# Transposing x on TensorE instead of by DMA in the first gate of a fused attention, experts and cosine-MLP kernel

## The chip, the cores and the metric

The kernel runs on one core of one Trainium2 chip. The metric is the time of one launch on the device, in microseconds (us): the median of a few runs. The kernel before took 1233.31 us (three runs, 1232.27 to 1233.43). A separate, profiled execution gives the trace.

## The reference

Three stages, each feeding the next. Cut to what matters:

```python
# attention: B, H, S, D = 4, 8, 576, 64; only the 32 largest scores of a row count
scores = scale * q @ k.T
kth    = 32nd largest of each row
attn   = softmax(where(scores >= kth, scores, -1e9))
x      = (attn @ v) as 2304 rows of 512
# experts: 8 of them, one per row, and only for rows with x @ w_skip > 0
e_idx  = argmax(x @ w_gate);  gate_w = softmax(x @ w_gate)[e_idx]
x2     = x + gate_w * (relu(x @ w1[e_idx]) @ w2[e_idx])      # other rows: x2 = x
# MLP: 512 -> 2048 -> 512
h      = x2 @ w_in
out    = (h * cos(h)) @ w_out
```

`w_in` and `w_out` come as 64-bit floats.

## The kernel before, in words

**Two halves.** The four batch entries are worked as two pairs, g = 0 and g = 1, of 1152 rows each. A pair has 8 heads of 9 *tiles* of 128 query rows: 72 tiles, numbered n = 0 to 143 over both pairs. Heads are taken from 7 down to 0 and inside a head the tile j from 8 down to 0. After a pair's attention come its gate (`route`), its experts (`experts`) and its share of the MLP (`cosine`).

**One tile** (`attend`). TensorE makes 128 x 576 scores into a two-bank PSUM slot (L584). VectorE takes the largest of eight pieces (L593) and narrows them (L603, L605); ScalarE makes exponentials and two helper passes (L610, L614, L617); TensorE shifts the scores twice (L622); VectorE finds the 32nd largest (L630) and masks (L633); ScalarE and GpSimd split the weights into two half-precision parts (L636, L640, L641); a DMA transposes them (L644, on SP's queue); TensorE multiplies with v (L651 to L660). Every third tile VectorE divides and writes three tiles' columns of x (L672 to L674). x is one buffer `xs` of three parts: part 2 holds j = 8, 7, 6, part 1 j = 5, 4, 3, part 0 j = 2, 1, 0. So part 0 is ready last.

**PSUM.** Pair 0 has three score slots, pair 1 two. The third slot, `s2`, is given up after its last tile, 71, and cut into two banks, `half`, which the experts and the MLP use (`recut`).

**Head preparation** (`prep_head`). q, k and v of the next head are loaded by DMA, multiplied by 16 on GpSimd (L520), split into two half-precision parts (ScalarE, and GpSimd at L496) and transposed by DMA (L525). GpSimd also works on the 64-bit weights `w_in`, `w_out` (L438, L445, L448) while pair 0's attention runs.

**The gate** (`route`). For each of nine row tiles, j = 0 to 8, x is split into two half-precision parts (`transposed`: L688 on ScalarE, L690 on VectorE), transposed by a DMA on SP's queue (L693), and TensorE makes nine logits (L743). Then one chain of small VectorE, ScalarE and TensorE instructions (L764 to L819) makes a table of rows for each expert.

**Experts.** GpSimd gathers 128 rows for an expert from `x_d` (L856), TensorE multiplies (pair 0: `turn` L868, `first` L888, `second` L919, in 32-bit precision; pair 1: half-precision parts made at L847 and L849). Each weight block is 512 KB and loaded on SP's queue (L839). Pair 0 has four buffers for them. The results are scattered into `x2_d` (L932). `store_x` writes x twice: to `x_d`, from which rows are gathered, and to `x2_d`, which holds x2.

**MLP** (`cosine`). For each of nine row tiles: 192 matmuls for h (L986), five elementwise steps (L998 to L1008), 48 matmuls for the output (L1016), an eviction (L1025). Pair 0's part, here cosine 0, is worked in between the attention of pair 1 and in what is left open by the gate and the experts of pair 1; cosine 1 comes last.

**What sets the order.** Every instruction group is a unit with an engine, an estimated cost, a priority and dependencies (`Plan.add`). `Plan.run` plays the units on a model of the engines: whichever engine is free takes the unit of least priority number among those that are ready in the model. The instructions are written in that order, and each engine then works strictly in it. A cost or a priority that changes can thus move instructions anywhere.

```python
                if ready[e]:
                    t = free[e]
                elif pending[e]:
                    t = max(free[e], pending[e][0][0])
...
            _, u = heapq.heappop(ready[e])
            u.fn()
```

## Time and profile before

| | |
|---|---|
| median of three runs | 1233.31 us |
| profiled execution, its own time | 1231.46 us |
| span of its instructions | 1229.3 us |
| TensorE busy | 965.1 us (79%) |
| VectorE busy | 875.2 us (71%) |
| ScalarE busy | 805.8 us (66%) |
| GpSimd busy | 598.8 us (49%) |

The span is what the trace covers; 2.2 us of the profiled execution lie around it. Busy shares are averages over stages with different limits. By the trace, pair 0's attention lasts to about 403 us, the first gate to 455 us, the first expert multiplication is at 462 us, pair 1's attention ends at 844 us, the experts of pair 1 at 1003 us, and cosine 1 fills the rest.

### The profile page before, as it was taken

To read this page: it belongs to the slowest core of one execution; us is meant where nothing else is said; L and a number is where in the kernel's file an instruction comes from. 1 tells how busy PE (TensorE), PEld (TensorE's weight loads), DVE (VectorE), ACT (ScalarE), POOL (GpSimd) and SP (SyncE) were. 2 spreads that over 40 slices of the span, in tenths; PEclk is the share of its full clock that TensorE was granted. 3 is DMA by queue.
4 is the path that set the end of the run, shared out by engine and by line. 5 is a ranking of instruction groups with operands and counts; after the bars stand their busy time and mean duration, and the time that the engine had idled before them with its cause. 6 is when DMAs were issued, how large, how long until landed. Compare 5 with 4: busy or idle time off the path is not lost.

```text
span 1229.3 us, 27654 instructions
## 1 busy us (share of the span) xinstructions
PE 965.1 (79%) x9855; PEld 681.8 (55%) x9856; DVE 875.2 (71%) x3186; ACT 805.8 (66%) x1657; POOL 598.8 (49%) x591
## 2 busy tenths in 40 slices
PE   1565565656565569898987989987999999999996
PEld 0343343333343357666654767765776667777773
DVE  6898998979897786777778878885478862433221
ACT  5888888878775656556666978775377755644431
POOL 6988979989654434444444633432222321122221
PEclk9985556555675559999996999999999999999999
DMA  7677687678669969999997455469379951310100
GB/s 184 148 164 166 130 156 162 146 146 163 112 113 245 202 130 222 256 271 280 267 283 195 96 105 133 88 151 239 72 223 336 302 191 38 70 35 19 26 20 21
DMA packets 352629, 193.81 MB, mean 158 GB/s; under 512 B 270050, under 2 KB 323298, under 8 KB 352480
## 3 DMA queue, kind: packets, MB, share of 16 engines
q1 hardware_dynamic: 349920, 185.66, 64.4%
q0 software_dynamic: 2560, 6.28, 1.6%
q8 instruction: 79, 1.29, 0.4%
q14 instruction: 70, 0.57, 0.1%
HBM read 107.50 MB, written 18.35 MB: 102 GB/s over the span
## 4 chain that ended last, share of the span: by engine, by line
PE 32%; DMA 16%; issue 9%; DVE 8%; POOL 6%; ACT 4%; SPq 2%; POOLq 0%; DVEq 0%; ACTq 0%
DMA arena<-arena 11%; PE half L986 5%; PE quarter L986 5%; PE quarter L1016 4%; PE m_bank L1016 4%; PE half L1016 3%; POOL arena L641 2%; DMA arena<-in_k_dram 1%; PE s L584 1%; DMA arena<-in_v_dram 1%; PE s L622 1%; PE m_bank L986 1%; DVE arena L633 1%; DMA arena<-x_d,gidx 1%; DVE arena L593 1%
## 5 line engine op out<-in xcount | busy, mean ns | idle before, releaser
L986 PEld LDWEIGHTS <-win 128*128 128x128 f16 x3456 | 215.7, 99 | 51.6 <-issue 1.8
L593 DVE MAX8 arena<-s 128x8 f32<-128x72 f32 x1152 | 197.6, 223 | 30.5 <-PE s L584 30.0
L1008 POOL TENSOR_TENSOR arena<-arena 128x512 f16<-128x512 f32 x72 | 86.5, 1201 | 254.6 <-ACT arena L1007 213.8
L651 PE MATMUL o_bank<-arena 128*128 128x65 f16 (+1 forms) x640 | 100.1, 221 | 99.2 <-DMA arena<-arena 96.0
L584 PE MATMUL s<-arena 128*128 128x320 f16 (+7 forms) x800 | 130.1, 328 | 52.4 <-DVE arena L633 33.6
L641 POOL TENSOR_TENSOR arena<-arena 128x512 f16<-128x512 f32 x144 | 169.8, 1179 | 0.0
L633 DVE SCALAR_TENSOR_TENSOR arena<-s,kth,arena 128x576 f32<-128x576 f32 x144 | 116.6, 809 | 50.9 <-PE s L622 38.5
L651 PEld LDWEIGHTS <-arena 128*128 128x128 f16 (+1 forms) x640 | 71.9, 116 | 144.5 <-DMA arena<-arena 133.5
L1003 DVE SCALAR_TENSOR_TENSOR arena<-arena 128x512 f32<-128x512 f32 x72 | 52.1, 723 | 136.6 <-ACT arena L1000 136.6
L986 PE MATMUL half<-arena,win 128*128 128x128 f16 x2112 | 146.7, 221 | 0.7 <-DMA arena<-arena 0.4
L636 ACT ACTIVATE arena<-arena 128x576 f16<-128x576 f32 x144 | 97.6, 678 | 73.4 <-DVE arena L633 56.3
L584 PEld LDWEIGHTS <-arena 128*128 128x128 f16 (+1 forms) x800 | 86.0, 122 | 98.0 <-issue 51.0
L640 POOL TENSOR_TENSOR arena<-arena 128x64 f16<-128x64 f32 x144 | 47.9, 332 | 164.1 <-ACT arena L636 148.0
L1016 PE MATMUL m_bank<-wout,arena 128*128 128x512 f16 x480 | 126.5, 381 | 0.0
L610 ACT ACTIVATE arena<-s,arena 128x576 f32<-128x576 f32 x144 | 105.4, 732 | 13.8 <-POOL arena L641 9.7
L622 PE MATMUL s<-arena,minus 128*128 128x320 bf16 (+1 forms) x288 | 76.5, 358 | 48.3 <-ACT arena L610 28.3
L630 DVE MAX8 kth<-s 128x8 f32<-128x584 f32 x144 | 110.0, 764 | 1.1
L614 ACT ACTIVATE arena<-s,arena 128x576 bf16<-128x576 f32 x144 | 105.7, 734 | 2.4
L520 POOL TENSOR_SCALAR arena<-arena 128x576 f32<-128x576 f32 (+1 forms) x45 | 77.2, 1717 | 61.5 <-DMA arena<-in_v_dram 34.4
L1016 PEld LDWEIGHTS <-arena 128*128 128x128 f16 x864 | 75.5, 98 | 48.5 <-issue 0.3
L622 PE MATMUL s<-arena,plus 128*128 128x320 bf16 (+1 forms) x288 | 77.3, 361 | 30.6 <-DVE kth L630 25.6
L653 PE MATMUL o_bank<-arena 128*128 128x64 f16 (+1 forms) x640 | 98.8, 218 | 0.0
(184 smaller groups left out, 2363.6 us busy)
## 6 DMA issues: line engine op xcount, KB each, us to landing
arena<-in_moe_w_dram SPq DMA_DIRECT2D x128, 512.0 KB
arena<-in_moe_w_in_dram SPq DMA_DIRECT2D x16, 512.0 KB
arena<-in_moe_w_out_dram SPq DMA_DIRECT2D x16, 512.0 KB
x_d<-arena SPq DMA_DIRECT2D x8, 768.0 KB
arena<-arena SPq DMA_DIRECT2D x32, 144.0 KB
arena<-x_d SPq DMA_DIRECT2D x18, 256.0 KB
out_dram<-arena SPq DMA_DIRECT2D x18, 256.0 KB
arena<-in_q_dram SPq DMA_DIRECT2D x16, 256.0 KB
```

Of the source, the lines that this page charges most:

```text
L584: nc.tensor.matmul(S_[rows, o:o + n_], qT.ap[:, i, cols], kT.ap[:, kc:kc + n_], start=(i == 0 and o < 512), stop=(i == 1), skip_group_chec ...
L593: add("DVE", dve(sw), lambda i=i: nc.vector.max(cand.ap[:, 8 * i:8 * i + 8], S_[:, sw * i:sw * i + sw]), r=[s], w=[cand[i]], prio=pr - 0.5)
L610: lambda: nc.scalar.activation(p.ap, S_, AF.Exp, bias=M[:, 40:41], scale=ESC),
L614: lambda: nc.scalar.activation(r.ap, S_, AF.Relu, bias=M[:, 41:42], scale=ESC),
L622: nc.tensor.matmul(S_[:, o:o + n_], by, r.ap[:, o:o + n_], start=False, stop=True, skip_group_check=True)
L630: add("DVE", 0.68, lambda: nc.vector.max(kth[g][:, z:z + 8], s.ap), r=[s], w=[found[n], in_turn], prio=pr)
L633: add("DVE", 0.73, lambda: nc.vector.scalar_tensor_tensor(p.ap, S_, kth[g][:, z + 7:z + 8], p.ap, op0=OP.is_ge, op1=OP.mult), r=[s, found[ ...
L641: nc.gpsimd.tensor_tensor(pc.ap[:, S + ST:], p.ap[:, 0:SM], pc.ap[:, 0:SM], op=OP.subtract)
L651: nc.tensor.matmul(oj[rows, 0:D + 1], pT.ap[:, c, rows], vh[:, 5 * b + c, :], start=(c == 0), stop=False)
L653: nc.tensor.matmul(oj[rows, 0:D], pT.ap[:, c, rows], vl[:, 5 * b + c, :], start=False, stop=False)
L986: nc.tensor.matmul(view(ph.ap, 4, P)[:, f, :], win.ap[:, c, sw, f0:f0 + P], xv[:, sx, c, :], start=(n == 0), stop=(n == 3 * KD - 1))
L1016: nc.tensor.matmul(po.ap, gv[:, sg, fc % 4, :], wout.ap[:, fc, sw, :], start=(fc == 0 and n_ == 0), stop=(fc == NFF - 1 and n_ == 2))
```

## The change

The gate of pair 0 no longer transposes by DMA. A new function `turned` transposes the 32-bit x on TensorE, four 128 x 128 blocks into one of the two banks of the third score slot (`ring_t`), and ScalarE and VectorE make the two half-precision parts from PSUM. For that the slot is recut before the gate instead of after it. Both gates take their row tiles from j = 8 down. The second store of x (`x2_d`) gets a larger priority number. The first four weight blocks of pair 0's experts wait for the division of tile 38 instead of tile 65. And the multiplication by 16 on GpSimd becomes a tensor-by-tensor product with a column of sixteens, with a planned cost of 1.23 us (0.11 + 576 x 0.00195) instead of 0.72 us.

```diff
+    ring_t = Ring(half)
...
+    times = sb("times", [1])
+    nc.vector.memset(times, SQ)
...
             if not early:
-                add("POOL", 0.2 + n * D * 0.0009, lambda: nc.gpsimd.tensor_scalar(x, x, SQ, None, op0=OP.mult),
-                    w=[st], prio=prio)
+                add("POOL", gp(n * D), lambda: nc.gpsimd.tensor_tensor(x, x, times[:, :, None].to_broadcast([P, n, D]),
+                                                                       op=OP.mult), w=[st], prio=prio)
...
+    def turned(src, src_slot, prio):
+
+        bk, xT = ring_t.new(), r_xT[0].new()
+        v16 = as16(xT.ap, 2, KD, P)
+
+        def turn():
+            for c in range(KD):
+                nc.tensor.transpose(view(bk.ap, KD, P)[:, c, :], src[:, c * P:(c + 1) * P], ident)
+
+        add("PE", 0.6, turn, r=[src_slot], w=[bk], prio=prio)
+        add("ACT", act(DM, True), lambda: nc.scalar.activation(v16[:, 0], view(bk.ap, KD, P), AF.Copy, scale=SX),
+            r=[bk], w=[xT], prio=prio)
+        add("DVE", dve(DM), lambda: nc.vector.scalar_tensor_tensor(
+            v16[:, 1], view(bk.ap, KD, P), SX, v16[:, 0], op0=OP.mult, op1=OP.subtract),
+            r=[bk], w=[xT], prio=prio)
+        return xT, v16
...
-                    prio=prio + (0.0 if dst is x_d[g] else 10.0))
+                    prio=prio + (0.0 if dst is x_d[g] else 30.0))
...
-        for j in range(NJ):
-            xT, xv = transposed(xs.ap[:, j, :], xs[j // 3], prio, g)
+        for j in reversed(range(NJ)):
+            if g == 0:
+                xT, xv = turned(xs.ap[:, j, :], xs[j // 3], prio)
+            else:
+                xT, xv = transposed(xs.ap[:, j, :], xs[j // 3], prio, g)
...
-                r=[gate[n0 - 7]] if g == 0 else [], w=[st], prio=prio[0] - 5, lat=0.6, dma=1.5)
+                r=[gate[n0 - 34]] if g == 0 else [], w=[st], prio=prio[0] - 5, lat=0.6, dma=1.5)
...
+    recut(third_ps, [s2], half, "half", "right")
     store_x(0, n0 + 0.0)
     route(0, n0 - 10.0)
-    recut(third_ps, [s2], half, "half", "right")
```

In the new file the lines after the insertions are larger by 1 to 23: L593 becomes L596, L633 L636, L674 L677, L644 L647, L707 L727, L847 L870, L998 L1021, L1025 L1048; the new L711 and L713 are the two evictions of `turned`.

VectorE's order at the end of pair 0, before. `s_82` is the third score slot, `s_77` and `s_78` the first two; `kth_126` belongs to pair 0, `kth_127` to pair 1. Tile 71 ends with the first row, parts 1 and 0 of x with the two L674, and L690 is the split of row tiles j = 0 and 1:

```order
L633 SCALAR_TENSOR_TENSOR arena<-s_82,kth_126,arena 128x576
...
L674 TENSOR_TENSOR arena<-o_bank,arena 128x3x64
...
L633 SCALAR_TENSOR_TENSOR arena<-s_77,kth_127,arena 128x576
...
L633 SCALAR_TENSOR_TENSOR arena<-s_78,kth_127,arena 128x576
...
L674 TENSOR_TENSOR arena<-o_bank,arena 128x3x64
...
L690 SCALAR_TENSOR_TENSOR arena<-arena 128x512 x2
```

The same place in the change, up to the first instruction of the routing table (L790):

```order
L677 TENSOR_TENSOR arena<-o_bank,arena 128x3x64
...
L636 SCALAR_TENSOR_TENSOR arena<-s_82,kth_128,arena 128x576
...
L713 SCALAR_TENSOR_TENSOR arena<-half_4389,arena 128x512
L713 SCALAR_TENSOR_TENSOR arena<-half_4390,arena 128x512
L636 SCALAR_TENSOR_TENSOR arena<-s_77,kth_129,arena 128x576
...
L636 SCALAR_TENSOR_TENSOR arena<-s_78,kth_129,arena 128x576
...
L677 TENSOR_TENSOR arena<-o_bank,arena 128x3x64
...
L790 TENSOR_SCALAR act_0_137<-lt_0_136 128x9
```

Six of the nine L713 now stand ahead of the division of part 0, and the last three, with the masks of tiles 74 and 75, between it and L790. In the order before the first expert multiplication on TensorE follows the scores of tile 83; in the change it follows those of tile 78.

SP's queue at the same place, before. The rows L644 are the transposes of tiles 70 to 73, `x_d_57` is the first store of x, `x_d` the second (`x2_d`):

```order
L644 DMA_TRANSPOSE arena<-arena 128x9x128
L707 DMA x_d_57<-arena 64x512 x2
L711 DMA x_d_57<-arena 128x512 x2
L644 DMA_TRANSPOSE arena<-arena 128x9x128
L707 DMA x_d<-arena 64x512 x2
L711 DMA x_d<-arena 128x512 x2
L644 DMA_TRANSPOSE arena<-arena 128x9x128
L716 DMA x_d_57<-arena 128x1536
L644 DMA_TRANSPOSE arena<-arena 128x9x128
L716 DMA x_d<-arena 128x1536
L693 DMA_TRANSPOSE arena<-arena 128x8x128 x2
```

And in the change, from tile 70's transpose on:

```order
L647 DMA_TRANSPOSE arena<-arena 128x9x128
L727 DMA x_d_57<-arena 64x512 x2
L731 DMA x_d_57<-arena 128x512 x2
L727 DMA x_d<-arena 64x512 x2
L731 DMA x_d<-arena 128x512 x2
L647 DMA_TRANSPOSE arena<-arena 128x9x128 x2
L736 DMA x_d_57<-arena 128x1536
L736 DMA x_d<-arena 128x1536
```

The second store of part 1 now stands ahead of tile 71's transpose, not behind it. The first four expert weight blocks stand between the transposes of tiles 67 and 70 before, and between those of tiles 39 and 41 in the change.

ScalarE's order behind the last split of an expert weight of pair 1 (L847, L870), where cosine 0 ends and cosine 1 begins, before (L998 starts the elementwise steps of a block of h, L688 splits a row tile of cosine 1, L1025 evicts a finished output):

```order
L847 ACTIVATE arena<-arena 128x1024 x3
L998 ACTIVATE arena<-half_4369 128x512
L1000 ACTIVATE arena<-arena,cbias 128x512
L1007 ACTIVATE arena<-arena 128x512
L998 ACTIVATE arena<-half_4368 128x512
...
L688 ACTIVATE arena<-arena 128x512 x2
...
L998 ACTIVATE arena<-half_4369 128x512
...
L1025 ACTIVATE arena<-m_bank 128x512
L1007 ACTIVATE arena<-arena 128x512
L1025 ACTIVATE arena<-m_bank 128x512
```

And in the change:

```order
L870 ACTIVATE arena<-arena 128x1024 x3
L691 ACTIVATE arena<-arena 128x512
L1048 ACTIVATE arena<-m_bank 128x512
L691 ACTIVATE arena<-arena 128x512
L468 ACTIVATE arena<-win_131 128x512 x3
```

Of cosine 0, three blocks of h and two outputs were still to do there; one output is left in the change. On TensorE the counts are 108 L986 and 78 L1016 behind the experts' last multiplication before, and no L986 and 39 L1016 in the change.

## Rows read from the trace of the kernel before

**Rows 1.** The page: span, TensorE's busy time, granted clock in 40 slices.

```profile
span 1229.3 us, 27654 instructions
PE 965.1 (79%) x9855; PEld 681.8 (55%) x9856; DVE 875.2 (71%) x3186; ACT 805.8 (66%) x1657; POOL 598.8 (49%) x591
PEclk9985556555675559999996999999999999999999
```

**Rows 2.** Windows: from:to, length, each engine's busy time (instructions), clock, DMA share, GB/s.

```profile
100.00:380.00 280.00, 168.29 (x1418) 108.34 (x1418) 250.78 (x1113) 226.01 (x524) 226.52 (x219) 0.60 0.73 150
388.00:462.00 74.00, 43.31 (x422) 30.26 (x423) 56.90 (x234) 40.85 (x87) 30.89 (x34) 0.52 0.82 173
462.00:650.00 188.00, 168.86 (x1436) 122.44 (x1435) 135.42 (x589) 115.40 (x252) 86.63 (x95) 0.99 1.04 261
650.00:840.00 190.00, 169.09 (x2095) 126.59 (x2094) 158.99 (x629) 147.69 (x318) 82.32 (x93) 0.95 0.60 133
840.00:1010.00 170.00, 158.85 (x1852) 115.24 (x1851) 120.17 (x158) 99.64 (x134) 42.32 (x29) 0.99 0.80 232
```

**Rows 3.** Source L633, one per tile, in 388:462 and 650:840; ns, first and last start.

```profile
L633 DVE SCALAR_TENSOR_TENSOR arena<-s,kth,arena x10: 816/818/818, 392.9 to 457.9; 128x576 f32<-128x576 f32 x10
L633 DVE SCALAR_TENSOR_TENSOR arena<-s,kth,arena x31: 796/817/819, 649.6 to 834.5; 128x576 f32<-128x576 f32 x31
```

**Rows 4.** Timeline of SP's queue at the end of pair 0: start, us, instruction.

```profile
375.12 1.85 SPq L839 DMA_DIRECT2D arena<-in_moe_w_dram  x2
...
387.75 0.57 SPq L839 DMA_DIRECT2D arena<-in_moe_w_dram  x1
...
394.33 1.21 SPq L707 DMA_DIRECT2D x_d<-arena  x2
...
396.81 1.42 SPq L644 DMA_TRANSPOSE arena<-arena  x1
398.27 1.85 SPq L707 DMA_DIRECT2D x_d<-arena  x2
400.17 1.07 SPq L711 DMA_DIRECT2D x_d<-arena  x2
...
407.76 3.97 SPq L693 DMA_TRANSPOSE arena<-arena  x2
...
433.93 1.45 SPq L693 DMA_TRANSPOSE arena<-arena  x1
```

**Rows 5.** Timeline of VectorE: tile 71's mask, part 0's division, the table's last instruction.

```profile
386.72 0.82 DVE L633 SCALAR_TENSOR_TENSOR arena<-s,kth,arena 128x576 f32<-128x576 f32 x1 [1.66 <-PE o_bank L660]
...
402.56 0.36 DVE L674 TENSOR_TENSOR arena<-o_bank,arena 128x192 f32<-128x192 f32 x1
...
454.96 0.16 DVE L819 TENSOR_SCALAR gs<-ts 128x8 f32<-128x8 f32 x1
```

**Rows 6.** Timeline: the last logits on TensorE, the table's first VectorE row, the first expert multiplication.

```profile
439.23 0.45 PE L743 MATMUL m_bank<-wg,arena 128*128 128x9 f16 x12
440.47 0.16 DVE L767 TENSOR_SCALAR act<-lt 128x9 f32<-128x9 f32 x1
462.24 0.98 PE L888 MATMUL half<-arena 128*128 128x128 f32 x5
```

**Rows 7.** Source L690: ns least/median/most, first and last start.

```profile
L690 DVE SCALAR_TENSOR_TENSOR arena<-arena x44: 666/692/1294, 404.1 to 1127.2; 128x512 f16<-128x512 f32 x44
```

**Rows 8.** Sources L520 and L445: two products on GpSimd, by a constant and by a tensor.

```profile
L520 POOL TENSOR_SCALAR arena<-arena x45: 1647/1654/1997, 18.2 to 687.8; 128x576 f32<-128x576 f32 x30, 128x640 f32<-128x640 f32 x15
L445 POOL TENSOR_TENSOR arena<-arena x32: 1256/1267/1748, 11.9 to 312.2; 128x512 f32<-128x512 f32 x32
```

**Rows 9.** Timeline of TensorE where pair 1's experts end and cosine 1 begins.

```profile
998.50 4.05 PE L919 MATMUL quarter<-arena 128*128 128x512 f16 x18
...
1015.07 2.17 PE L986 MATMUL quarter<-arena,win 128*128 128x128 f16 x36
1017.08 10.52 PE L1016 MATMUL m_bank<-wout,arena 128*128 128x512 f16 x48
```

## The prediction

> **What bounds the kernel now.** I read the page first, then busy times by stage, then the pace of the tiles, then the timelines of the two places that the change touches. TensorE's granted clock stands at 5 to 6 tenths for most of the first third and drops back to 5 around slices 12 to 14, then is full [rows 1]. By stage [rows 2]: while pair 0's attention runs (100 to 380 us) VectorE is busy 250.78 of 280 us (90%) and GpSimd 226.52 (81%), so these two set the pace and TensorE waits for them. [...] So the gate is a bridge on which all later TensorE work waits. Tiles pass it at (457.9 - 392.9) / 9 = 7.2 us each, against (834.5 - 649.6) / 30 = 6.16 us beside cosine 0 [rows 3].
>
> Why the bridge is long: its first DMA transpose is issued at 407.76, the last at 433.93 [rows 4], mixed with tiles' own transposes. It starts late because it begins with j = 0, which lies in part 0, and part 0 is divided only at 402.56, 16 us after tile 71's mask [rows 5]. Logits end at 439.68, the table at 455.12, the first expert multiplication starts at 462.24 [rows 5, 6].
>
> **The change part by part.**
>
> *The gate.* Removed: nine DMA transposes on SP. Added: 36 transposes on TensorE, nine evictions each on ScalarE and VectorE in place of the splits that were there; I price an L713 as an L690, 0.69 us [rows 7]. A TensorE transpose in 32 bits has its nearest row in L888, 0.98 us for five, so 36 are about 7 us; TensorE idles 31 of 74 us there [rows 2], so I cost them at nothing, and at most 7 us if that cover went. With j descending, six row tiles need only parts 2 and 1. Their six evictions (4.2 us) fit between tile 71's mask at 386.7 and part 0's division. That division I leave at 402.6: four weight blocks are gone from SP's queue ahead of it (issues of 0.57 to 1.85 us [rows 4]), but the second store of part 1, whose issues take 1.85 + 1.07 = 2.9 us, now goes ahead of tile 71's transpose. So the second store is in the written order not put behind, the larger number notwithstanding. Bounds: 398 (the weights' issues saved, no harm from the store) to 409 (the store's issues, and as much again in transfer).
>
> From part 0's division to the table's first instruction VectorE has about a tile and a half of attention and three L713 left. A tile costs it at most 135.42 / 32 = 4.2 us [rows 2] (32 masks fall in that window), so 1.5 x 4.2 + 2.1 = 8.4 us, at 77 to 90% busy some 10 us: 413. The table's chain from there is unchanged, 440.47 to 455.12 = 14.65 us, and so is the way to the experts, 7.1 us [rows 5, 6]. The first expert multiplication comes at 413 + 14.65 + 7.1 = 434.8, 27 us sooner; with the bounds above and 77 against 95% busy, 20 to 33.
>
> *What is given back.* The order shows that the experts now start behind the scores of tile 78 instead of 83: five tiles more have to run beside experts and cosine 0. From then on TensorE's order has nearly the same amount of other work per tile, so I let these tiles pass at the pace of the later stage: 5 x 6.16 = 30.8 us. So pair 1's attention ends no sooner: 27 - 30.8, **about 4 us later**. What is won is work done beside it: by tile 143 the order has 144 L986 and 39 L1016 of cosine 0 more behind it.
>
> *The end.* From tile 143 to the last expert multiplication of pair 1 both orders give TensorE nearly the same work. Behind that, cosine 0 had 108 L986 and 78 L1016 left before, 39 L1016 now. Before, the experts' last multiplications end at 1002.55 and cosine 1's first h starts at 1015.07, 12.5 us later, the time of scatter, load, split and transpose, filled with cosine 0; after two microseconds of it the last 48 L1016 of cosine 0 follow, 10.52 us [rows 9]. Now 39 x 0.22 = 8.5 us fill the 12.5, 4 us stay open, and the 10.5 us are gone. 36 L986 fewer inside pair 1's experts (2.2 us, less 0.65 for three L1016 more) give another 1.5: **12 us gained**.
>
> *The product on GpSimd.* 45 times L520 at 1.65 us becomes a product of two tensors. The nearest row is L445, in place and in 32 bits, 1.267 us for 512 columns, so 1.43 for 576: 0.22 us less, for the 21 of pair 0 4.7 us of GpSimd's time [rows 8]. No row has a repeated operand, so it may be slower too: the longest L520, 2.0 us, gives 7 us lost. GpSimd is busy 81% there beside VectorE at 90%, so I take a third of the gain, 1.5 us. The new planned cost, and the weights moved to tiles 39 to 41, rearrange pair 0's stage throughout; in the order the steps of each head stand within a tile or three of where they were. I cost that at nothing, within 5 us to either side.
>
> [...]
>
> *The first four weights* are issued by 387.75 [rows 4] and used from 462.24: sooner gains nothing by itself.
>
> **Sum.** 12 gained at the end, 4 given back, 1.5 on GpSimd: 9.5 us off the profiled execution's 1231.46, so 1222. That execution stands 1.85 below the median of 1233.31; against the median I say **1223 us**.
>
> **Rivals.**
>
> *A, more is gained (about 1210).* The tiles of the later stage are paced not by TensorE but by waits that the change also shortens. For it: TensorE is busy 89%, not 100 [rows 2]. If 32 tiles beside cosine 0 ran 0.25 us faster each (4% of 6.16), 8 us more; with the upper bound of the bridge, 33, 6 more: 1223 - 14 = 1209. Against it: in-order TensorE, and VectorE at 84% there.
>
> *B, no change (about 1231).* GpSimd's new product takes the 2.0 us of its upper bound, 7 us lost instead of 1.5 gained, all of it ahead of the bridge: 1223 + 8.5 = 1231.5. Or the bridge shrinks by 20 instead of 27, its lower bound: 1223 + 7 = 1230. It decides when the new product's median is over 1.9 us or part 0's division comes at 409. The first needs every microsecond of GpSimd to be on the path, where it is busy 81%. [...]
>
> *C, slower (about 1238).* Tile 71's transpose lands late. On SP it now stands behind both stores of part 1, and its result gates part 0, whose division stands in VectorE's order ahead of the work of tiles 74 and 75, and whose transposes stand in TensorE's order ahead of their shifts. So a late part 0 stops all engines. The second store is 0.77 MB, both are 1.5; at the 173 GB/s of that window [rows 2] the two take 9 us, at half of that, with tiles' transposes between, 18. If 15 us of it fall ahead of the transpose, the bridge shrinks by 12 only: 1223 + 15 = 1238. It decides from a division at about 412, where nothing is left of the gain. Against it: the transpose is issued at 396.81 and used at 402 already behind one store [rows 4, 5], and the weights' 2 MB are gone from just there.
>
> *D, the change doesn't do what it says*: true of the second store and idle for the weights, as said; the transposes on TensorE do stand in the order, so the main part holds.
>
> **How the numbers follow.** Forecast 0.58 (1214 to 1229), A 0.17, B 0.12, C 0.13. A measurement here can tell about 0.2%, 2.5 us. Faster by more: forecast and A, 0.75; within 0.2%: B, 0.12; slower: C, 0.13. The range leaves out the far ends of A and C: 1206 to 1235; the forecast's own is 1214 to 1229.
>
> **What would show it.** In the new trace: six L713 before part 0's division, at about 402; the table's end near 428, the first expert multiplication near 435; tile 143's mask within a few us of 834.5; an open stretch of some 4 us on TensorE between the last expert multiplication and cosine 1; cosine 1 starting some 10 us sooner; the new product near 1.43 us. Wrong if tile 143 moves by over 8 us, if part 0 is divided after 409, or if pair 0's last mask moves by more than 5 us from 386.7.

## Result and the profile after

The change takes **1203.57 us** (median of four runs, 1202.71 to 1204.25) against 1232.79 for the kernel before, measured beside it: ratio 0.9764, 95% interval 0.9752 to 0.9777, 29 us faster. The prediction said 1223 and a range of 1206 to 1235: the direction was right, the size was not, and the time lies outside the range. The profiled execution took 1203.05, its span is 1200.8.

The page of the change, for [rows 1]:

```profile
span 1200.8 us, 27693 instructions
...
PE 968.3 (81%) x9891; PEld 689.2 (57%) x9892; DVE 878.0 (73%) x3187; ACT 803.6 (67%) x1657; POOL 576.5 (48%) x591
...
PEclk9999996555657699999978999999999999999999
```

TensorE's granted clock stays high for six slices here, where it fell after three before. That is not where the time comes from: this execution has a mean clock of 0.907, the three others of the same kernel 0.857 and 0.858, and all four times lie within 1.6 us.

VectorE's timeline around the gate, for [rows 5]; L636 is the mask, L677 a division, L713 the new eviction, L790 the table's first instruction, L842 its last:

```profile
369.15 0.36 DVE L677 TENSOR_TENSOR arena<-o_bank,arena 128x192 f32<-128x192 f32 x1
369.71 0.80 DVE L636 SCALAR_TENSOR_TENSOR arena<-s,kth,arena 128x576 f32<-128x576 f32 x1
372.54 1.35 DVE L713 SCALAR_TENSOR_TENSOR arena<-half,arena 128x512 f16<-128x512 f32 x2
...
384.18 0.36 DVE L677 TENSOR_TENSOR arena<-o_bank,arena 128x192 f32<-128x192 f32 x1
...
392.59 0.15 DVE L790 TENSOR_SCALAR act<-lt 128x9 f32<-128x9 f32 x1
...
405.88 0.17 DVE L842 TENSOR_SCALAR gs<-ts 128x8 f32<-128x8 f32 x1
```

And TensorE's, for [rows 6] and [rows 9]: the first expert multiplication, then the place where the experts of pair 1 end (L942) and cosine 1 begins (L1009), with what is left of cosine 0 (39 L1039) between:

```profile
413.45 1.28 PE L911 MATMUL half<-arena 128*128 128x128 f32 x10
...
982.04 4.05 PE L942 MATMUL quarter<-arena 128*128 128x512 f16 x18
985.93 8.58 PE L1039 MATMUL m_bank<-wout,arena 128*128 128x512 f16 x39
...
997.59 0.83 PE L1009 MATMUL quarter<-arena,win 128*128 128x128 f16 x12
```

Source L636, one mask per tile, beside the experts and beside cosine 0, for [rows 3]:

```profile
L636 DVE SCALAR_TENSOR_TENSOR arena<-s,kth,arena x34: 800/818/819, 413.7 to 619.2; 128x576 f32<-128x576 f32 x34
...
L636 DVE SCALAR_TENSOR_TENSOR arena<-s,kth,arena x33: 796/817/819, 622.6 to 817.9; 128x576 f32<-128x576 f32 x33
```

The span is 28.5 us shorter; three pieces of it hold 28.2:

| piece | before | after | difference | predicted |
|---|---|---|---|---|
| start to the mask of tile 71 | 386.7 | 369.7 | -17.0 | -1.5 |
| that mask to the mask of tile 143 | 447.8 | 448.2 | +0.4 | +4 |
| that mask to the last output of cosine 1 | 384.3 | 372.7 | -11.6 | -12 |

The gate's two pieces came out as worked out. The piece ahead of the gate, which the prediction put at 1.5 us, holds more than half of the gain. VectorE there (windows from the mask of tile 8 to that of tile 71, first before, then the change):

```profile
74.50:386.70 312.20, 187.05 (x1577) 120.59 (x1574) 280.18 (x1238) 252.92 (x584) 251.65 (x243) 0.60 0.72 150
```

```profile
66.50:369.70 303.20, 192.08 (x1572) 124.34 (x1572) 284.54 (x1247) 255.52 (x596) 248.44 (x247) 0.74 0.75 163
```

VectorE did as much work (280.18 and 284.54 us) and was idle for 18.7 us instead of 32.0; the window is 9.0 us shorter. The other 8.0 us are gained ahead of tile 8's mask. GpSimd's product, source L523, for [rows 8]:

```profile
L523 POOL TENSOR_TENSOR arena<-arena,times x45: 1142/1148/1727, 18.0 to 675.7; 128x576 f32<-128x576 f32 x30, 128x640 f32<-128x640 f32 x15
```

1.148 us where 1.43 was forecast: 0.51 us less for each. Ahead of tile 71's mask there are 28 of them in both kernels, not the 21 that the prediction counted, since pair 1's first heads are prepared there too. In the kernel before:

```profile
L520 POOL TENSOR_SCALAR arena<-arena x28: 1647/1680/1997, 18.2 to 371.5; 128x576 f32<-128x576 f32 x19, 128x640 f32<-128x640 f32 x9
```

That makes 28 x 0.51 = 14 us of GpSimd's time in pair 0.

### The profile page after: what moved, and what is told of

It is laid out like the page before. It is cut to its first block, busy times and chain, and to the rows that moved or that the text cites. A ratio compares the mean times of both kernels' runs of the same rounds, so it can differ in the third digit from the quotient of the medians.

```text
span 1200.8 us, 27693 instructions
## 1 busy us (share of the span) xinstructions
PE 968.3 (81%) x9891; PEld 689.2 (57%) x9892; DVE 878.0 (73%) x3187; ACT 803.6 (67%) x1657; POOL 576.5 (48%) x591
## 5 line engine op out<-in xcount | busy, mean ns | idle before, releaser
L1009 PEld LDWEIGHTS <-win 128*128 128x128 f16 x3456 | 216.5, 99 | 49.8 <-issue 1.7
L596 DVE MAX8 arena<-s 128x8 f32<-128x72 f32 x1152 | 197.0, 224 | 26.7 <-PE s L587 26.3
L644 POOL TENSOR_TENSOR arena<-arena 128x512 f16<-128x512 f32 x144 | 170.3, 1183 | 0.0
L654 PE MATMUL o_bank<-arena 128*128 128x65 f16 (+1 forms) x640 | 99.2, 221 | 76.4 <-DMA arena<-arena 72.5
L636 DVE SCALAR_TENSOR_TENSOR arena<-s,kth,arena 128x576 f32<-128x576 f32 x144 | 116.5, 809 | 48.4 <-PE s L625 41.8
L1009 PE MATMUL half<-arena,win 128*128 128x128 f16 x2112 | 147.9, 222 | 0.0
L1026 DVE SCALAR_TENSOR_TENSOR arena<-arena 128x512 f32<-128x512 f32 x72 | 51.6, 717 | 124.4 <-ACT arena L1023 124.4
L654 PEld LDWEIGHTS <-arena 128*128 128x128 f16 (+1 forms) x640 | 71.9, 117 | 118.4 <-DMA arena<-arena 107.8
L643 POOL TENSOR_TENSOR arena<-arena 128x64 f16<-128x64 f32 x144 | 50.7, 352 | 184.4 <-ACT arena L639 169.5
L1039 PE MATMUL m_bank<-wout,arena 128*128 128x512 f16 x480 | 126.8, 381 | 1.1 <-ACT arena L1048 0.9
L625 PE MATMUL s<-arena,plus 128*128 128x320 bf16 (+1 forms) x288 | 76.7, 359 | 44.1 <-DVE kth L633 40.4
L633 DVE MAX8 kth<-s 128x8 f32<-128x584 f32 x144 | 110.1, 765 | 1.2
L1039 PEld LDWEIGHTS <-arena 128*128 128x128 f16 x864 | 75.2, 98 | 48.5 <-issue 1.7
L606 DVE MAX8 arena<-arena 128x8 f32<-128x64 f32 x432 | 94.5, 219 | 6.3
L620 ACT ACTIVATE arena<-arena 128x576 bf16<-128x576 bf16 x144 | 97.4, 677 | 1.2
```

The costliest lines, as they stand in the source:

```text
L596: add("DVE", dve(sw), lambda i=i: nc.vector.max(cand.ap[:, 8 * i:8 * i + 8], S_[:, sw * i:sw * i + sw]), r=[s], w=[cand[i]], prio=pr - 0.5)
L633: add("DVE", 0.68, lambda: nc.vector.max(kth[g][:, z:z + 8], s.ap), r=[s], w=[found[n], in_turn], prio=pr)
L636: add("DVE", 0.73, lambda: nc.vector.scalar_tensor_tensor(p.ap, S_, kth[g][:, z + 7:z + 8], p.ap, op0=OP.is_ge, op1=OP.mult), r=[s, found[ ...
L644: nc.gpsimd.tensor_tensor(pc.ap[:, S + ST:], p.ap[:, 0:SM], pc.ap[:, 0:SM], op=OP.subtract)
L654: nc.tensor.matmul(oj[rows, 0:D + 1], pT.ap[:, c, rows], vh[:, 5 * b + c, :], start=(c == 0), stop=False)
L1009: nc.tensor.matmul(view(ph.ap, 4, P)[:, f, :], win.ap[:, c, sw, f0:f0 + P], xv[:, sx, c, :], start=(n == 0), stop=(n == 3 * KD - 1))
```

## Experiments

Two theories first. **I:** the quicker product frees GpSimd. **II:** the new planned cost changes the order. Neither was meant to be large in the prediction. All ratios are to the kernel before on the same chip, with 95% intervals; not all experiments ran on the same chip. The table after the sixth experiment collects what the profiles show.

**Product alone, cost alone** (in the kernel before).

```diff
+    times = sb("times", [1])
+    nc.vector.memset(times, SQ)
...
-                add("POOL", 0.2 + n * D * 0.0009, lambda: nc.gpsimd.tensor_scalar(x, x, SQ, None, op0=OP.mult),
-                    w=[st], prio=prio)
+                add("POOL", 0.2 + n * D * 0.0009, lambda: nc.gpsimd.tensor_tensor(x, x, times[:, :, None].to_broadcast([P, n, D]),
...
```

> The kernel before with one instruction changed: GpSimd multiplies q, k and v by a repeated column of sixteens, planned at the old cost, so that every engine keeps its order. Theory I (the shorter product itself: 0.50 us less, 21 times ahead of tile 71, on an engine that with VectorE paces pair 0) expects most of the 17 us: tile 71's mask at 370 to 376 instead of 386.7, time 1216 to 1222 us. Theory II (the new planned cost gives pair 0 a better order) expects at most 3 us from this: 1229 to 1232. Theory III (the 17 us come from the weights and the gate taken out of the end of pair 0) expects none: 1231 to 1234.

Measured: 1221.96, ratio 0.9909 (0.9883 to 0.9936). The order is that of the kernel before, so all of it is the shorter instruction. Tile 71's mask comes at 378.8, 7.9 us sooner, which is less than theory I expected (370 to 376).

```diff
-                add("POOL", 0.2 + n * D * 0.0009, lambda: nc.gpsimd.tensor_scalar(
+                add("POOL", gp(n * D), lambda: nc.gpsimd.tensor_scalar(
```

> The kernel before with the old product but its planned cost raised from 0.72 to 1.23 us, which moves instructions on all engines. Theory I expects 1229 to 1236 us, tile 71's mask within 4 us of 386.7. Theory II expects 1215 to 1221 and the mask near 372. Theory III expects no change.

Measured: 1222.37, ratio 0.9918 (0.9890 to 0.9947). No instruction is quicker here, and pair 0's last mask comes at 368.0 instead of 386.7: the order alone does that. Of those 18.7 us 8.8 are lost again behind the mask (last column of the table). Both theories hold, for 10 to 11 us each.

**The rest of the change.** The gate with TensorE's transposes, the early recut and j descending, without the early weights, the later second store, the product and its cost:

> The kernel before with the first gate's transposes on TensorE, the earlier recut and j descending; the product, its cost, the weights' release and the store's priority as before. By the accounting of the prediction (bridge some 30 us shorter, five tiles given back at 6.16 us, 12 us won at the end) 1219 to 1226 us, tile 71's mask where it was. If the gate also gave the 17 us of pair 0: 1203 to 1208.

Measured: 1227.59, ratio 0.9938 (0.9908 to 0.9968), with tile 71's mask at 388.0. And the whole change but for the product and its cost:

> The changed kernel with the old product and its old planned cost: gate, weights and store as changed. Theories I and II expect what the gate gives alone, 1218 to 1226 us, and tile 71's mask within 4 us of 386.7. Theory III expects the weights' release to show: mask near 370 to 375 and 1203 to 1210.

Measured: 1223.53, ratio 0.9923 (0.9896 to 0.9950), 9.5 us. This is the part for which the prediction had 12 - 4 = 8. It leaves 0.9923 - 0.9764, about 20 us, to product and cost together. Tile 71's mask stays at 389.1, so theory III, by which the weights or the gate had freed the end of pair 0, falls. The second store's priority, the early recut and the second gate's reversal have no run of their own.

**How those 20 us divide in the changed kernel.** Old product with the new cost, new product with the old cost:

> The changed kernel with the old multiplication by a constant, but with its new planned cost of 1.23 us. The runs so far: the change 1203.6, the change without product and cost 1223.5, so product and cost together are worth 20 us there; in the kernel before each alone gave 11 to 12, and the mask of tile 71 came 18.7 us sooner by the cost alone and 7.9 by the product alone. Theory O (the planned cost puts GpSimd's work into a better order, and once VectorE is busy 93 per cent in pair 0 the quicker product is covered): 1204 to 1208, mask of tile 71 within 3 us of 369.7. Theory S (both add up, about 10 each): 1211 to 1215, mask of tile 71 at 376 to 381. Theory P (the quicker product carries it, the order by itself is worth nothing in this kernel): 1219 to 1224.

Measured: 1209.22, ratio 0.9825 (0.9786 to 0.9863).

> The changed kernel with the new product, but planned at the old cost of 0.72 us. Theory O: 1212 to 1217, mask of tile 71 at 380 to 384 (the 7.9 us that the product alone gave in the kernel before). Theory S: 1211 to 1215. Theory P: 1203 to 1207, mask of tile 71 within 3 us of 369.7. So this run tells P from the others, and the run with the old multiplication and the new cost tells O from S.

Measured: 1216.97, ratio 0.9881 (0.9846 to 0.9916). From 0.9923 the cost alone brings 0.0098 (12 us), the product alone 0.0042 (5 us); with the other in place already 0.0117 (14 us) and 0.0061 (7.5 us). Theory P is out; what was found lies between O and S: the order carries about two thirds. By the intervals each of these differences is uncertain by some 5 us. The order's share is clear of that; of the product's, 5 us is not and 7.5 only just.

What the profiles show, of one execution each (that of `gate_only` took 7 us more than its median, that of `no_product` 9). The columns: the start of tile 71's mask; VectorE's idle time from tile 8's mask to tile 71's (length of the window less its busy time); in the same window, the wait for a DMA ahead of the first weight load of the multiplication by v (L651, L654 in the change); from tile 71's mask to the last output. All in us.

| kernel | ratio | mask 71 | VectorE idle | wait for DMA | to the end |
|---|---|---|---|---|---|
| before | 1 | 386.7 | 32.0 | 73.3 | 832.1 |
| op_only | 0.9909 | 378.8 | 25.9 | 65.5 | 832.1 |
| cost_only | 0.9918 | 368.0 | 15.2 | 49.7 | 840.9 |
| cost_true | 0.9926 | 375.0 | 22.2 | 56.4 | 833.6 |
| reversed_only | 0.9967 | 388.1 | 30.1 | 71.7 | 824.1 |
| weights_only | 0.9958 | 391.6 | 33.4 | 76.6 | 824.7 |
| gate_only | 0.9938 | 388.0 | 31.2 | 73.1 | 834.4 |
| no_product | 0.9923 | 389.1 | 30.5 | 76.3 | 831.8 |
| after_op | 0.9881 | 383.6 | 30.4 | 75.9 | 822.9 |
| after_cost | 0.9825 | 377.3 | 21.2 | 53.5 | 817.5 |
| the change | 0.9764 | 369.7 | 18.7 | 48.5 | 820.9 |
| the change, again | 0.9791 | 369.8 | 16.6 | 49.2 | 828.8 |
| after_row | 0.9744 | 375.5 | 19.6 | 51.6 | 818.7 |
| after_gp | 0.9812 | 373.3 | 19.3 | 38.0 | 823.0 |
| after_dve | 0.9883 | 386.7 | 32.4 | 66.2 | 816.4 |
| after_c095 | 0.9852 | 378.5 | 22.8 | 50.4 | 819.4 |
| after_c160 | 0.9740 | 370.5 | 19.0 | 49.0 | 814.2 |
| c160_again | 0.9730 | 372.7 | 21.1 | 51.7 | 819.8 |
| after_dma | 0.9760 | 373.4 | 19.0 | 50.5 | 814.9 |
| dma_c160 | 0.9821 | 373.3 | 19.5 | 51.1 | 829.8 |

Read down the third to fifth columns: with the old planned cost, whatever else is changed, the wait for DMA is 65 to 77 us and VectorE idles 26 to 33; with a new one 38 to 56 and 15 to 23, but for `after_dve`, in which other costs are changed too. The waiting rows themselves, groups of instructions by line in that window: busy, mean | idle ahead of it and who ended it. The kernel before, then the same instructions in the new order (`cost_only`):

```profile
L633 DVE SCALAR_TENSOR_TENSOR arena<-s,kth,arena 128x576 f32<-128x576 f32 x63 | 50.7, 804 | 9.8 <-PE s L622 7.3 <-POOL wout L448 1.8 <-POOL arena L496 0.4
...
L651 PEld LDWEIGHTS <-arena 128*128 128x128 f16 (+1 forms) x278 | 34.9, 127 | 81.1 <-DMA arena<-arena 73.3 <-issue 4.0
```

```profile
L633 DVE SCALAR_TENSOR_TENSOR arena<-s,kth,arena 128x576 f32<-128x576 f32 x63 | 50.6, 804 | 2.8 <-PE s L622 1.4 <-POOL arena L641 1.3
...
L651 PEld LDWEIGHTS <-arena 128*128 128x128 f16 (+1 forms) x272 | 34.6, 129 | 55.2 <-DMA arena<-arena 49.7 <-issue 2.3
```

The whole change but product and cost:

```profile
L634 DVE SCALAR_TENSOR_TENSOR arena<-s,kth,arena 128x576 f32<-128x576 f32 x63 | 50.8, 806 | 10.1 <-PE s L623 9.6 <-POOL arena L521 0.3 <-issue 0.2
...
L652 PEld LDWEIGHTS <-arena 128*128 128x128 f16 (+1 forms) x282 | 35.9, 128 | 83.3 <-DMA arena<-arena 76.3 <-issue 3.5
```

The change with the old product, so with the new order and GpSimd as slow as before:

```profile
L634 DVE SCALAR_TENSOR_TENSOR arena<-s,kth,arena 128x576 f32<-128x576 f32 x63 | 50.5, 804 | 2.8 <-PE s L623 1.4 <-POOL arena L642 0.9 <-issue 0.4
...
L652 PEld LDWEIGHTS <-arena 128*128 128x128 f16 (+1 forms) x278 | 35.8, 130 | 59.3 <-DMA arena<-arena 53.5 <-issue 2.0
```

The change with the new product at the old planned cost:

```profile
L636 DVE SCALAR_TENSOR_TENSOR arena<-s,kth,arena 128x576 f32<-128x576 f32 x63 | 50.7, 804 | 10.9 <-PE s L625 7.9 <-POOL wout L451 3.0
...
L654 PEld LDWEIGHTS <-arena 128*128 128x128 f16 (+1 forms) x278 | 35.5, 129 | 82.6 <-DMA arena<-arena 75.9 <-issue 3.2
```

And the change itself:

```profile
L636 DVE SCALAR_TENSOR_TENSOR arena<-s,kth,arena 128x576 f32<-128x576 f32 x63 | 50.6, 804 | 1.6 <-PE s L625 1.4
...
L654 PEld LDWEIGHTS <-arena 128*128 128x128 f16 (+1 forms) x278 | 35.8, 130 | 54.1 <-DMA arena<-arena 48.5 <-issue 1.6
```

With the old order TensorE stands for longer at a multiplication by v whose transposed weights are not there yet: 73 to 76 us, against 49 to 54 with the new one. In its order the shifts of later tiles (L622, L623, L625) come behind that, and VectorE's masks wait for those: of the 9.8 to 10.9 us idle ahead of the masks 7.3 to 9.6 ended with a shift, with the new order 1.4 of 1.6 to 2.8. These six are the cleanest rows of it; the idle time of the masks alone does not order all kernels (`after_c095` has 10.4 us there and is quicker than `after_op`). The transposes do come sooner: from the start of a tile's mask to the issue of its transpose it takes, on average over tiles 9 to 71, 4.36 us in `after_cost` against 4.66 in `no_product`, and 4.23 in the change against 4.57 in `after_op`. That is 19 to 21 us over 63 tiles. It is not the whole of it: `op_only`, in the old order, has 4.55 against 4.81 before, and its wait for DMA fell by 7.8 us only.

Ahead of tile 8's mask the new order acts in another way: less work stands there. The kernel before and `cost_only`, from the start to that mask (columns as in [rows 2]):

```profile
0.00:74.50 74.50, 29.21 (x205) 18.20 (x207) 56.97 (x227) 52.10 (x116) 59.80 (x63) 1.00 0.77 171
```

```profile
0.00:68.30 68.30, 27.94 (x210) 17.12 (x212) 51.28 (x219) 48.33 (x108) 54.76 (x59) 0.72 0.77 174
```

GpSimd, the busiest engine there, has four instructions fewer (a product by 16 and three steps on the 64-bit weights), VectorE eight. Tile 8's mask comes 6.2 us sooner by the cost alone, 2.0 by the quicker product alone (72.5), and 8.0 in the change.

**Is a truer planned cost the reason?** The old multiplication planned at what it takes, in the kernel before:

```diff
-                add("POOL", 0.2 + n * D * 0.0009, lambda: nc.gpsimd.tensor_scalar(
+                add("POOL", 0.2 + n * D * 0.00255, lambda: nc.gpsimd.tensor_scalar(
```

> The kernel before with its old multiplication, planned at what it takes: 1.67 us for 576 columns, 1.83 for 640 (0.72 before, 1.23 gave 1222.4). Theory T (the nearer a planned cost is to the measured one, the better the order): 1216 to 1222, mask of tile 71 at 368 or sooner. Theory L (any other order does it by luck, the order before happened to be a bad one): anywhere from 1218 to 1235, with no relation to the cost. Theory of the ready time (0.72 was so low that the plan put work in front of what GpSimd had not done yet, and past 1.2 nothing more is to be had): 1220 to 1225, mask of tile 71 at 367 to 371.

Measured: 1221.74, ratio 0.9926 (0.9910 to 0.9943): as good as 1.23, not better. Tile 71's mask is at 375.0, later than with 1.23 (368.0) and outside what theory T and that of the ready time expected. Then all of GpSimd's costs that are planned by columns, in the changed kernel, `0.22 + n * 0.002` for `0.11 + n * 0.00195` (the product's own becomes 1.37):

> The changed kernel with all GpSimd tensor operations planned at 0.22 + 0.002 us a column in place of 0.11 + 0.00195: 0.35 for 64 (measured 0.35), 1.24 for 512 (measured 1.17 to 1.38), 1.37 for 576 (measured 1.16 and 1.32). Theory T: a few us better, 1197 to 1203, since most of GpSimd's planned costs are too low by 0.1 to 0.2 us. Theory of the ready time and theory O: no more to be had from GpSimd, 1201 to 1207. Theory L: 1198 to 1220.

Measured: 1208.48, ratio 0.9812 (0.9795 to 0.9830), slower than the change, and outside all ranges but theory L's. And VectorE's two steps on the 64-bit weights:

```diff
-        add("DVE", 0.34, lambda: nc.vector.tensor_scalar(ti, words[:, :, 1], 3, None,
+        add("DVE", 0.85, lambda: nc.vector.tensor_scalar(ti, words[:, :, 1], 3, None,
...
-        add("DVE", 0.6, lambda: nc.vector.scalar_tensor_tensor(ti, words[:, :, 0], 29, ti,
+        add("DVE", 1.0, lambda: nc.vector.scalar_tensor_tensor(ti, words[:, :, 0], 29, ti,
```

> The changed kernel with VectorE's two steps on the 64-bit weights planned at what they take there: 0.85 and 1.0 us instead of 0.34 and 0.60 (the trace has 0.94 and 1.02 on average). Theory T (planned costs nearer to the measured ones give a better order; for GpSimd's other operations it failed, 1208.5 against 1203.6): VectorE is busy 93 per cent in pair 0, so here it should count: 1196 to 1202. Theory L (it is the one wrong cost that was harmful, not the rest): 1201 to 1210.

Measured: 1216.08, ratio 0.9883 (0.9833 to 0.9932): 12 to 15 us worse, all of it ahead of tile 71's mask. That is outside the ranges of both theories. So theory T falls. Truer costs do not make a better order in general. Other planned costs for the product alone, 0.95 and 1.60 us for 576 columns (`gp(n * D) - 0.28` and `+ 0.37`):

> The changed kernel with the product planned at 0.95 us for 576 columns instead of 1.23 (0.72 gave 1217.0). Theory K (a planned cost well below the real one lets the plan put work too early, so that TensorE waits for transposed weights; the nearer to the real 1.16 the better, and flat above): 1206 to 1212, VectorE's idle time ahead of the masks of tiles 9 to 71 between 3 and 9 us (1.6 in the change, 10.9 at 0.72). Theory L (every planned cost gives another order, good or bad by luck): 1198 to 1222 with no relation to the cost.

Measured: 1212.04, ratio 0.9852 (0.9825 to 0.9880). The time is at the upper end of theory K's range, but the idle time ahead of the masks is 10.4 us, not 3 to 9: that step of theory K was missed.

> The changed kernel with the product planned at 1.60 us for 576 columns instead of 1.23. Theory K: 1202 to 1208, VectorE's idle time ahead of the masks of tiles 9 to 71 under 4 us, as at 1.23. Theory L: 1198 to 1222.

Measured: 1198.80, ratio 0.9740 (0.9707 to 0.9773). As theory K has it, the ratio falls from 0.9881 (0.72) by 0.9852 (0.95) to 0.9764 (1.23), and is 0.9740 at 1.60, a little better than flat and below theory K's range of times. For this one cost, too low was harmful and too high was not, in these runs. Theory L is not excluded by four points: its range holds them all, and the orders of `after_gp` and `after_dve` show that other costs move the time as far. Why a larger planned cost gives the better order is not shown.

A second measurement of this version on another chip:

> The changed kernel with the product planned at 1.60 us, a second time. As ratios to the kernel before: the change had 0.976 on one chip and 0.979 on another, this version 0.974. Theory H in part (with this order the transposes on TensorE are worth their 8 us or so): ratio 0.972 to 0.976, so 1196 to 1202. Theory G (they are worth nothing, what differed was the chip): 0.979 to 0.983, the ratio of the version without them being 0.982.

Measured: 1199.76, ratio 0.9730 (0.9708 to 0.9752). Both measurements are the lowest ratios found, some 3 to 4 us below the change's first ratio; the intervals touch or overlap. Both are clearly below the kernel before.

**What makes the product quick.** A row of 64 sixteens, repeated over the row groups, as second operand:

```diff
-    times = sb("times", [1])
+    times = sb("times", [D])
...
-                add("POOL", gp(n * D), lambda: nc.gpsimd.tensor_tensor(x, x, times[:, :, None].to_broadcast([P, n, D]),
+                add("POOL", gp(n * D), lambda: nc.gpsimd.tensor_tensor(x, x, times[:, None, :].to_broadcast([P, n, D]),
```

> The changed kernel, but the second operand of GpSimd's product is a row of 64 sixteens repeated over the 9 or 10 row groups, in place of a single sixteen repeated over all. Theory R (the product is quick because one operand is the same element again and again): 1.25 to 1.45 us for 576 columns (the rate of the products with two full operands, 1.27 for 512), time 1204 to 1209. Theory F (any product of two tensors takes this long here, the slow form is that by a constant): 1.14 to 1.19 us, time 1201 to 1206.

Its source row:

```profile
L523 POOL TENSOR_TENSOR arena<-arena,times x45: 1388/1407/2146, 17.6 to 678.0; 128x576 f32<-128x576 f32 x30, 128x640 f32<-128x640 f32 x15
```

1.407 us: with an operand that changes from element to element, the forecast's 1.43 would have been nearly right. The single repeated sixteen is worth another 0.26 us, as theory R has it; why the product by a constant is the slowest of the three, no run shows. The time was 1202.99 (1197.27 to 1208.36), ratio 0.9744 (0.9695 to 0.9793), 1 us below theory R's range: those 0.26 us are not seen in it.

**The gate's parts.** Only the order of the row tiles, still by DMA (`for j in reversed(range(NJ))` for g = 0):

> The kernel before with one edit: the first gate takes its row tiles from j = 8 down, still transposed by DMA. Theory D (the bridge was long because the gate began with the part of x that is ready last): most of the 32 us by which the bridge from the mask of tile 71 to the first expert multiplication shrank in the change (75.5 to 43.8 us) is here too, bridge 48 to 58 us. Theory Q (it was long because nine transposes wait in SP's queue between the tiles' own): bridge 65 to 75 us. Time by either 1224 to 1232, since a shorter bridge is mostly given back by pair 1's attention.

Measured: 1227.39, ratio 0.9967 (0.9940 to 0.9993). The bridge is 63.7 us, against 75.5 before and 43.7 in the change: theory Q's side, if not its range. Only the early weights (`gate[n0 - 34]`):

> The kernel before with one edit: the first four expert weight blocks wait for tile 38 instead of tile 65. The prediction says idle by itself: 1229 to 1235, mask of tile 71 within 5 us of 386.7. Rival (their 2 MB in the way of the last tiles of pair 0 cost time there): 1222 to 1228, mask of tile 71 at 378 to 382.

Measured: 1228.24, ratio 0.9958 (0.9938 to 0.9978): some 5 us faster (3 to 8 by the interval), though pair 0's last mask comes no sooner (391.6, as the prediction's idle weights would have it). The time lies between the two ranges. In the profile the gain is behind that mask: the bridge is 69.7 us, and from tile 143's mask to the last output it takes 379.4 us instead of 384.3. Which part of the other plan does this is not shown. Only the transposes on TensorE taken back, `transposed` in place of `turned`, in the change:

> The changed kernel, but the first gate's nine row tiles are transposed by DMA as before, from j = 8 down; everything else is as in the change. Theory G (a shorter bridge is given back by pair 1's attention, so the transposes on TensorE are worth only what lies open at the end): 1204 to 1208, bridge from the mask of tile 71 to the first expert multiplication 58 to 66 us (63.7 where only the order was reversed in the kernel before, 43.8 in the change). Rival H (20 us of bridge are worth half their length, since TensorE ends with less of cosine 0 left): 1211 to 1216.

Measured: 1201.81, ratio 0.9760 (0.9726 to 0.9795), with a bridge of 434.73 - 373.36 = 61.4 us. That is the change's own ratio without its first item, and 2 us below theory G's range. Then, on one chip, the change again and the same edit together with 1.60 us planned:

> The changed kernel itself, on the same chip as the next run: 1201 to 1206 if the level of this chip is that of the first one. It is the measure for the next run.

Measured: 1209.97, ratio 0.9791 (0.9753 to 0.9829): 4 us above the range expected, so the level is not that of the first chip.

> The changed kernel with the product planned at 1.60 us and the first gate's row tiles transposed by DMA, from j = 8 down. Theory G (the transposes on TensorE are worth nothing by themselves): within 3 us of the 1198.8 that the version with TensorE's transposes and 1.60 us gave, so some 3 to 7 us below the changed kernel on this chip. Rival H (they are worth half the bridge that they save, some 8 us): 1205 to 1209.

Measured: 1212.89, ratio 0.9821 (0.9787 to 0.9855), where 1.60 us with the transposes on TensorE had 0.973 to 0.974. It is slower than both theories expected. So beside one order the 17.6 us of bridge that TensorE's transposes save are worth nothing that can be measured, beside another about 0.8%, 10 us; but that pair was not measured on one chip, and the change itself had 0.0027 more on the chip of `dma_c160`, 3 us.

From tile 143's mask to the last output the profiles agree better. With the transposes on TensorE it takes 370.4 to 374.1 us in all twelve of them: 372.7 and 373.8 in the change, 370.4 and 370.8 with 1.60 us. With DMA it takes 375.9 in `after_dma` and 377.5 in `dma_c160`, and 378.8 to 386.0 in the other six. So at the end the transposes are worth some 2 to 7 us. What lies between the masks of tiles 71 and 143 hides it: it took 439 to 460 us, and 448.2 and 455.1 in two profiles of the change. Where those differences come from stays open. The whole later part of the change moves as far from one execution to another: tile 71's mask at 369.7 and 369.8, and 820.9 and 828.8 us from there to the end. Differences of that size in the last column say nothing by themselves.

## Why the prediction was wrong, point by point

**What bounds pair 0: read right, used wrongly.** VectorE at 90% leaves 10% of the 280 us [rows 2], so some 29 us of waiting that a better order or a quicker feeder could take. The prediction named VectorE and GpSimd as the pair that sets the pace and then priced what changes both at next to nothing.

**The step that failed is "The product on GpSimd".** First, "The new planned cost ... I cost that at nothing, within 5 us to either side". It was worth 12 to 14 us in this kernel and 10 in the one before. That each head's steps stand within three tiles of where they were was true and no argument: by such small shifts TensorE's wait for transposed weights went from 73 to 50 us in `cost_only`, and tile 8's mask came 6.2 us sooner. Second, the product was priced at 1.43 us and took 1.15, since no row had a repeated operand, and 28 of them stand in pair 0, not 21. Third, "I take a third of the gain": of those 14 us of GpSimd's time 5 to 7.5 were gained in the changed kernel, a third to a half, and some 11 in the kernel before (ratio 0.9909). With the 20 us that product and cost are worth together in place of 1.5, the sum of 9.5 would have been 28. (The sum's last step is off by one: 1233.31 - 9.5 is 1224, not 1223.)

Two of the prediction's own signs of being wrong came: pair 0's last mask moved by 17.0 us, where 5 were allowed, and tile 143's by 16.6 (834.5 to 817.9), where 8 were. Both are the one gain ahead of the gate.

**The bridge: right.** That the gate is a bridge rests on the busy shares of [rows 2]: in it VectorE 77% and TensorE 59%, at a granted clock of 0.52, and behind it TensorE 90, 89 and 93%, at 0.95 or more. Predicted 27 us shorter, measured 31.8 (75.5 to 43.7). Part 0's division came 14.5 us after tile 71's mask (15.8 before), from there to the table's first instruction 8.4 us (10 predicted), the table took 13.5 (14.65). The 36 transposes took 7.35 us of TensorE in all (7 estimated). Part of their row:

```profile
370.76 1.77 PE L708 MATMUL half<-ident,arena 128*128 128x128 f32 x8
373.61 0.64 PE L708 MATMUL half<-ident,arena 128*128 128x128 f32 x4
```

**Given back: right.** The bridge became 31.8 us shorter and pair 1's attention, counted from tile 71's mask, 0.4 us longer (7.3 in the second profile of the change; 4 predicted): everything given back, five tiles more beside experts and cosine 0, as the order said. Over all profiles this stretch does not follow the bridge: 443 to 460 us with a bridge of 42 to 48 us, 439 to 455 with one of 58 to 79.

**The end: right in the trace.** 8.58 us of cosine 0 stand between the experts and cosine 1, 3 us stay open (4 predicted), 11.6 us are gained (12), 10.5 in the second profile. By the runs, product and cost apart, the change is worth 9.5 us (8 predicted). What the prediction had wrong about it is the share of the transposes: tested alone in the kernel before, the mere reversal brings 4 us (1 to 7) and the weights that it called idle 5 (3 to 8); in the changed kernels the transposes on TensorE add between nothing and 10.

**The rivals.** A's 1209 is nearest in number, but not by its mechanism: tiles beside cosine 0 pass at (817.9 - 622.6) / 32 = 6.10 us, against 6.16, 2 us in all where A wanted 8. Its upper bound of the bridge nearly came (31.8 us, where A had 33), but was given back. B's product over 1.9 us did not come (its median is 1.148). C's late transpose neither, though both stores of part 1 do stand ahead of it. SP's queue in the change (L727 and L731 are the stores, L647 a transpose):

```profile
372.20 1.07 SPq L731 DMA_DIRECT2D x_d<-arena  x2
373.32 1.11 SPq L727 DMA_DIRECT2D x_d<-arena  x2
374.47 1.40 SPq L731 DMA_DIRECT2D x_d<-arena  x2
376.04 3.38 SPq L647 DMA_TRANSPOSE arena<-arena  x2
```

The division at 384.18 is 8 us behind that issue, where it was 6 before (396.81 to 402.56); but the issue itself came 6.3 us after tile 71's mask, where it was 10.1. D held for the second store.

**The range** was too narrow on the fast side because the re-plan was given 5 us where nothing in the trace bounded it. The edits of planned costs made here moved the time by 3 to 15 us, up or down.

## What to carry to other kernels

Where a planner writes the order, a planned cost is an edit of the whole stage: price it not at zero but by the idle time of the engine that sets the pace there, here 32 us. That bounds what a better order can win there; nothing here bounds what a worse one can lose. Ask of each wait in such a stage what feeds it, and try a single planned cost that is far below its row in the trace, tested alone: it won 10 us for GpSimd's product and lost 12 to 15 for VectorE's two steps. And a part of the change that gives it its name may be worth the least: take it out of the finished version, not only put it into the old one.

## What was not expected of the hardware

On GpSimd a 32-bit product of 576 columns in place took 1.65 us by a constant, 1.41 with a row of 64 values as second tensor, and 1.15 with one value repeated (medians of 45, of which 15 have 640 columns). These are durations in the profile; from the start of a product of 576 columns to the start of GpSimd's next instruction, where nothing idles between, the medians are 1.73 us by a constant (the kernel before) and 1.10 with one value repeated (the change).

A higher granted clock in pair 0 brought nothing that shows. The window from tile 8's mask to tile 71's in the second profile of the change has 0.58 (the third column from the right), where the first had 0.74; tile 71's mask came at 369.8 and 369.7. In both TensorE stands for 49 us in that window waiting for transposed weights:

```profile
65.90:369.80 303.90, 188.91 (x1572) 122.47 (x1572) 287.33 (x1248) 256.00 (x596) 248.47 (x247) 0.58 0.75 162
```
